# Long causal convolution beside attention: kv stationary in four column tiles, filter rows moving

## The chip, the cores and the metric

The kernel runs on one core of a Trainium2 chip. The metric is the device time of one execution in microseconds (us), the median of several runs. Every experiment is measured on the same chip as fresh runs of the kernel before.

## The reference, cut to what matters

Two independent branches are computed and laid side by side.

```python
# A (H3-style): short convolution of k, times v, then a causal convolution over all 2048 steps
for t in range(4):
    k_shift = k_shift + k_pad[:, t:t + S, :] * shift_k[:, 3 - t]
kv = k_shift * v                                   # [2048, 640]
y = irfft(rfft(kv_pad) * rfft(ssm_k_pad))[:S]      # y[s] = sum_r kv[r] * ssm_k[s - r], each of 640 channels
a = q * (y + kv * ssm_D)
# B: full (not causal) attention, 32 heads of 20, with its projections
p = softmax((q @ k.T) * 20 ** -0.5);  b = (p @ v) @ wo
out = concat([a, b], -1)                           # [1, 2048, 1280]
```

## The kernel before

The program is straight-line code. A planner in Python, with an assumed cost for each operation, orders the instructions of all engines at build time: attention is the frame, the projections and the convolution are put into gaps that the planner sees on TensorE.

The exponentials are shared between ScalarE (two or three score tiles an instruction) and VectorE (one tile as a chain of five instructions), which gets a tile when its planned backlog is short:

```python
def EXP_task(k, m, vec, b0, got):                       # m tiles on ScalarE, vec (0 or 1) on VectorE
    P.op("act", lambda e: e.activation(P_sb[:, s0:s0 + m, :], ..., ACT.Exp, scale=scale), ...)
    if vec:
        chain_start(k + m, b0 + m, got[m])
def want_vec(k, now):
    if not 60 < k < NU - 34 or len(chains) >= NXB or not xfree: return 0
    if ((k + 2) // 4) % NKB > 13 or micro_late(now - 1.5): return 0
    return int(max(0.0, P.T["dve"] - now) + backlog() < VQ)
```

The convolution is a set of matmuls with a Toeplitz matrix. One filter tile `HK` serves four channels; its columns are the stationary operand and kv, spread over zeros by GpSimd, moves. The cost in the code is what the planner assumes; in the trace of this kernel the convolution's matmuls start 25 ns apart at 8 columns, 29 at 64 and 55 at 128 (medians at full clock):

```python
def hk_load(qd):      # 4 transfers of 32 partitions, one 4224-byte run each
    P.dmas("sp", [(HK[...][32 * X:32 * X + 32], ap(kext, [[1, 32], [1, HKW]], ...)) for X in range(4)], ...)
def kvx_build(c):     # 80 copies in all
    P.op("pool", lambda e: e.tensor_copy(dst, src), ...)
def conv_task(bt):    # 40 tasks of 4 x 32 matmuls
    lhsT = HK[sl][:, 64 + 128 * d - 32 * r1:64 + 128 * d - 32 * r1 + 128]   # 128 neighbouring elements
    rhs = sub(KVX[i], [[128, 2], [1, n]], ...)                              # 8 to 128 columns
    cost = max(0.025, 2 * n / 2400 + 0.0025)
    # [...] then three VectorE instructions to take the sums out
```

The softmax here doesn't subtract the row's maximum and nothing guards it: scores larger than these inputs give would overflow.

## Time and profile before

| | kernel before |
|---|---|
| time, three runs | 893.14 us median (888.44 to 895.65) |
| span of the profiled run | 889.3 us |
| ScalarE busy with exponentials / idle just before them | 851.5 / 19.1 us |
| VectorE chains of five instructions | 171 |
| TensorE instructions | 11,432 weight loads, 11,432 matmuls |
| half clock after 213 us (the trace's clock records) | 24 us |

"Idle" stands in the last column of a group's line: the time that the engine had nothing to do just before instructions of this group. A group that grows in busy time with the same count has slower instructions; a group that grows in idle time is waiting. Three groups from the page of the kernel before, to be held against the same groups later; other lines are in the prediction:

```profile
L639 ACT ACTIVATE P_sb<-PS 128x1536 bf16<-128x1536 f32 (+1 forms) x729 | 851.5, 1417 | 19.1 <-PE PS L597 18.4
...
L931 PEld LDWEIGHTS PS<-R 128*128 128x128 bf16 x5120 | 197.7, 97 | 108.9 <-issue 108.5
...
L668 DVE SCALAR_TENSOR_TENSOR XZ<-XI 128x512 f32<-128x512 uint16 x171 | 123.0, 719 | 0.4
```

### The profile page before, as it was taken

The numbers are of one execution on the slowest core, as the hardware profiler recorded it, in microseconds if no ns is written. First come the engines' busy times: TensorE is split into PE (matmuls) and PEld (weight loads), VectorE is DVE, ScalarE is ACT, GpSimd is POOL, SyncE is SP. The second block draws the span as 40 slices with busy tenths as digits, with TensorE's granted clock in tenths as the row PEclk, the third lists the DMA queues.
The fourth block names the chain that finished last, engine by engine and source line by source line (L and its number), as shares of the span: only waits on it lengthen the run. The fifth ranks groups of instructions, "written<-read, shape, count | busy, mean of one in ns | idle before, by whom it ended". The sixth has DMA issues, their size and how long they took to land.

```text
span 889.3 us, 26279 instructions
## 1 busy us (share of the span) xinstructions
PE 835.4 (94%) x11432; PEld 388.0 (44%) x11432; DVE 785.4 (88%) x1427; ACT 856.0 (96%) x737; POOL 126.5 (14%) x94
## 2 busy tenths in 40 slices
PE   9999889998999999998999999999989999999987
PEld 5432223222455554544545454444545445454322
DVE  4569999999699999998999999899999999999752
ACT  6699999999799999998999999999999999999996
POOL 3000000001522021210220220122022012200000
PEclk9999999999699999999999999999999999999999
DMA  9614233335666675553579656675644546355141
GB/s 301 202 56 153 93 116 105 105 105 90 158 176 175 176 191 140 158 138 99 161 161 180 162 162 187 177 210 146 169 131 131 163 130 190 110 162 145 32 107 56
DMA packets 83598, 129.15 MB, mean 145 GB/s; under 512 B 34561, under 2 KB 60283, under 8 KB 83483
## 3 DMA queue, kind: packets, MB, share of 16 engines
q1 hardware_dynamic: 81323, 124.36, 51.0%
q0 software_dynamic: 704, 2.74, 1.0%
q8 instruction: 90, 1.47, 0.7%
q10 hardware_dynamic: 1456, 0.37, 0.2%
q14 instruction: 25, 0.20, 0.1%
HBM read 116.81 MB, written 13.23 MB: 146 GB/s over the span
## 4 chain that ended last, share of the span: by engine, by line
ACT 48%; DVE 30%; PE 20%; issue 1%; DVEq 0%
ACT P_sb L639 48%; PE PS L931 7%; PE PS L597 6%; DVE P_sb L673 5%; DVE XI L666 5%; DVE XZ L668 5%; DVE XZ L671 5%; DVE XI L670 4%; PE PS L692 3%; PE PS L445 2%; DVE R L952 1%; PE PS L348 1%; DVE ZS L950 1%; DVE ZS L949 1%; DVE OT_sb L702 1%
## 5 line engine op out<-in xcount | busy, mean ns | idle before, releaser
L639 ACT ACTIVATE P_sb<-PS 128x1536 bf16<-128x1536 f32 (+1 forms) x729 | 851.5, 1417 | 19.1 <-PE PS L597 18.4
L597 PE MATMUL PS<-QT,KT 20*128 20x512 bf16 x2048 | 286.5, 388 | 30.6 <-ACT P_sb L639 21.7
L931 PE MATMUL PS<-R 128*128 128x128 bf16 (+15 forms) x5120 | 245.1, 194 | 3.6 <-DVE R L952 2.5
L931 PEld LDWEIGHTS PS<-R 128*128 128x128 bf16 x5120 | 197.7, 97 | 108.9 <-issue 108.5
L692 PE MATMUL PS<-P_sb,V_sb 128*21 128x512 bf16 x2048 | 173.5, 388 | 6.0 <-DVE P_sb L673 4.8
L901 POOL COPY R<-R 32x512 bf16<-32x512 bf16 x80 | 114.9, 1436 | 443.7 <-PE PS L931 431.3
L597 PEld LDWEIGHTS PS<-QT,KT 20*128 20x128 bf16 x2048 | 70.7, 91 | 200.1 <-ACT P_sb L639 153.8
L666 DVE TENSOR_SCALAR XI<-PS 128x512 int32<-128x512 f32 x171 | 117.0, 684 | 17.4 <-PE PS L597 16.8
L671 DVE SCALAR_TENSOR_TENSOR XZ<-XZ,XI 128x512 f32<-128x512 f32 x171 | 128.1, 749 | 0.0
L673 DVE SCALAR_TENSOR_TENSOR P_sb<-XZ,XI 128x512 uint16<-128x512 f32 x171 | 120.9, 707 | 4.9
L668 DVE SCALAR_TENSOR_TENSOR XZ<-XI 128x512 f32<-128x512 uint16 x171 | 123.0, 719 | 0.4
L670 DVE TENSOR_SCALAR XI<-XI 128x512 int16<-128x512 int16 x171 | 93.2, 545 | 0.0
L692 PEld LDWEIGHTS PS<-P_sb,V_sb 128*21 128x21 bf16 x2048 | 37.6, 89 | 79.4 <-issue 50.4
L348 PE MATMUL PS<-Zt 128*128 128x512 bf16 x208 | 63.6, 402 | 1.5 <-DVE Zt L342 1.0
L530 DVE TENSOR_TENSOR R<-R 128x640 bf16<-128x640 bf16 x128 | 61.6, 487 | 3.7 <-DMA R<-in_A_v_dram 0.9
L445 PE MATMUL PS<-xT,WQ 128*20 128x512 bf16 (+1 forms) x660 | 48.9, 385 | 3.6 <-DVE R L952 1.7
L445 PE MATMUL PS<-xT,R 128*20 128x512 bf16 (+2 forms) x660 | 44.8, 374 | 0.2
L702 DVE CAST OT_sb<-PS 128x512 bf16<-128x512 f32 x32 | 21.9, 685 | 14.5 <-PE PS L692 14.2
L503 PE MATMUL PS<-R,xT 128*128 128x160 bf16 (+1 forms) x240 | 31.2, 257 | 1.6 <-ACT P_sb L639 0.8
L431 DVE CAST KT<-PS 128x512 bf16<-128x512 f32 (+1 forms) x32 | 21.4, 673 | 11.1 <-PE PS L445 11.1
L878 POOL MEMSET R<- 128x2048 bf16 x2 | 3.8, 1900 | 190.7 <-DMA kvr_scratch<-R 190.6
L431 DVE CAST QT<-PS 128x512 bf16<-128x512 f32 (+1 forms) x32 | 21.6, 676 | 6.3 <-PE PS L445 6.2
(52 smaller groups left out, 302.0 us busy)
## 6 DMA issues: line engine op xcount, KB each, us to landing
R<-kext_scratch SPq DMA_DIRECT2D x640, 132.0 KB, 3.0
R<-in_A_k_dram SPq DMA_DIRECT2D x15, 640.0 KB, 3.9
kext_scratch<-in_A_ssm_k_dram POOLq DMA_DIRECT2D x1, 2560.0 KB, 14.7
R<-in_A_v_dram SPq DMA_DIRECT2D x16, 160.0 KB, 5.4
kv_scratch<-R SPq DMA_DIRECT2D x16, 160.0 KB
kvr_scratch<-R SPq DMA_DIRECT2D x16, 160.0 KB
R<-kvr_scratch SPq DMA_DIRECT2D x8, 320.0 KB, 7.0
R<-in_A_q_dram SPq DMA_DIRECT2D x32, 80.0 KB, 2.0
```

What stands on the lines that cost most here:

```text
L348: P.op("pe", lambda e: e.matmul(bank[bk], Zt, zrhs, start=start, stop=start, skip_group_check=True), reads=[b_Zt], writes=[bkb[bk]], tok=s ...
L445: ins = e.matmul(bank[bk][32 * i:32 * i + DH, 0:n], Wt[:, cc, off + i * DH:off + (i + 1) * DH], xT[:, cc, x0:x0 + n], start=(cc == 0), sto ...
L597: ins = e.matmul(bank[b0 + i], KT[32 * u:32 * u + DH, g, kb * 128:(kb + 1) * 128], QT[32 * u:32 * u + DH, qs(qc, g), :], start=True, stop= ...
L639: P.op("act", lambda e: e.activation(P_sb[:, s0:s0 + m, :], PS[:, b0 * 512:(b0 + m) * 512].rearrange("p (u q) -> p u q", u=m), ACT.Exp, sc ...
L666: (lambda e: e.tensor_scalar(XI, bank[bk], scale * 1.4426950408889634 * w, 127.0 * w, op0=ALU.mult, op1=ALU.add), [bkb[bk]], [bl, bh], 0.6 ...
L668: (lambda e: e.scalar_tensor_tensor(XZ, u, w * c2 / c3, u, op0=ALU.add, op1=ALU.mult), [bl], [bz], 0.69, True),
L670: (lambda e: e.tensor_scalar(hi, hi, 128.0, None, op0=ALU.mult), [bh], [bh], 0.456, True),
L671: (lambda e: e.scalar_tensor_tensor(XZ, XZ, w * w * c1 / c3, u, op0=ALU.add, op1=ALU.mult), [bl, bz], [bz], 0.69, True),
L673: (lambda e: e.scalar_tensor_tensor(P_sb[:, z, :].bitcast(U16), XZ, 128.0 * c3 / w ** 3, hi, op0=ALU.mult, op1=ALU.add), [bh, bz], [b_P[z] ...
L692: ins = e.matmul(bank[OBANK][32 * u:32 * u + DH + 1, :], V_sb[:, kb, 4 * g + u, :], P_sb[:, slot[4 * b + u], :], start=first, stop=last, t ...
L901: P.op("pool", lambda e, dst=dst, src=src: e.tensor_copy(dst, src), reads=[cv["KVr"]], writes=[cv["KVX"][i]] if X == 3 else [], extra=(cv[ ...
L931: P.op("pe", lambda e, o=o, lhsT=lhsT, rhs=rhs, st=st, last=last: e.matmul(o, lhsT, rhs, start=st, stop=last, skip_group_check=True), read ...
```

## The change

The intent: the convolution loads 128x128 weights 5120 times for only 8 to 128 moving columns each, GpSimd's copies cost VectorE time (L671 takes 753 ns in the mean from 240 to 830 us and 679 from 780 to 830, where GpSimd rests), and taking sums out costs three VectorE instructions a task. So the operation is turned round: kv becomes the stationary operand, 32 columns for one channel, four channels in the four column tiles of the array; 64-column pieces of the filter rows move. Four far offsets of 512 steps fill the 128 rows of the contraction. GpSimd's copies go, sums leave by one copy, a transpose and one addition, and gating is done inside each task. The diff cut to its core (`[...]` marks cuts):

```diff
+HKW = 544
+NHK = 3
+CB, NJ, J0, NT = 64, 78, 14, 20
+CQ = 0.03
+PVMIN, TIGHT = 3, 9
[...]
-        def kvx_build(c):                     # GpSimd's copies
[...]
+        def kva_load(b):
+            P.dmas("sp", [(sub(KVA, [[2 * CB, 64 - 16 * a], [1, CB]], (J0 + 16 * a) * 2 * CB + CB * h, 32 * a, 32),
+                           ap(kvr_d, [[D, 32], [32 * D, 64 - 16 * a], [1, CB]], h * D // 2 + b * CB))
+                          for a in range(4) for h in range(2)], d_kva, reads=b_kvd, writes=[cv["KVA"]])
+        def hk_load(gi):                      # 4 transfers, runs of 1088 bytes
+            P.dmas("sp", [(HK[i][32 * a:32 * a + 32].rearrange("p (c x) -> p c x", c=8),
+                           ap(kext, [[1, 32], [KXL, 8], [1, HKW]], [...] + 512 * a)) for a in range(4)], [...])
+        def conv_task(t):                     # 20 tasks x 4 x 2 x 16 groups
+                            for j in range(4):
+                                ins = e.matmul(
+                                    bank[bk][32 * j:32 * j + 32, (2 * v + h) * 64:(2 * v + h) * 64 + 64],
+                                    sub(KVA, [[4 * CB, 32]], (J0 - 2 * d + r) * 2 * CB + h * CB + t % 4 * 16 + 4 * v + j),
+                                    HK[i][:, (4 * w + j) * HKW + 64 * d - 32 * r + 32:(4 * w + j) * HKW + 64 * d - 32 * r + 96],
+                                    start=st, stop=sp, tile_position=(0, 32 * j), skip_group_check=True)
+                        P.op("pe", pe, reads=rd, writes=[bkb[bk]], tok=last, c=CQ, st=64 / 2400, kind="pv")
+            [...] copy to SBUF, Y_task: transpose, add kv * D, multiply by q
-                m = min(len(ok), 2 if slack < 1.0 else 3)
+                m = min(len(ok), max(1, int((slack + 0.1) / 0.22)))
```

In `sub(KVA, [[4 * CB, 32]], ...)` the 32 weights of a tile lie 4 x 64 = 256 elements, 512 bytes, apart. In `KVA` the channels lie side by side, because that is how kv can be transferred in runs of 128 bytes.

More of the change, by code (lines that the diff above doesn't have):

```diff
@@ L23 @@
 KXL = S + KPAD
-HKW = 2112
-NHK = 4
+HKW = 544
+NHK = 3
+CB, NJ, J0, NT = 64, 78, 14, 20
 NPU = 24
@@ L275, in build_kernel @@
         Wo_sb = sb("Wo_sb", [128, NCC, D])
-        Dbc = sb("Dbc", [128, D])
+        Dh = sb("Dh", [128, D // 2])
         ident = sb("ident", [128, 128])
-        ZS = sb("ZS", [128, 256], FP32)
         rden = sb("rden", [128, 32], FP32)
-        HK_E, KVR_E, KVX_E, Y_E, AST_E = HKW, 64 * 80, 8 * 256, 16 * 320, 320
+        HK_E, KVA_E, A_E = 8 * HKW, NJ * 2 * CB, 32 * CB
         ph0 = NCC * 2 * D + 4 * 4 * D + 2 * 5 * D + KS * D + 2 * D + 2 * D
-        ph1 = NHK * HK_E + KVR_E + 2 * KVX_E + 2 * Y_E + 5 * AST_E
+        ph1 = NHK * HK_E + KVA_E + 2 * 512 + 2 * A_E
         xT = sb("xT", [128, NCC, S])
@@ L301, in build_kernel @@
         HK = [carve(HK_E) for _ in range(NHK)]
-        KVr = carve(KVR_E).rearrange("p (j c) -> p j c", j=64)
-        KVX = [carve(KVX_E) for _ in range(2)]
-        Y = [carve(Y_E).rearrange("p (t c) -> p t c", t=16) for _ in range(2)]
-        Aq = [carve(AST_E) for _ in range(3)]
-        Akv = [carve(AST_E) for _ in range(2)]
+        KVA = carve(KVA_E)
+        Ys = [carve(512) for _ in range(2)]
+        Akv, Aq = carve(A_E), carve(A_E)
         PS = E(nc.psum_tensor("PS", [128, 4096], FP32))[:, :]
@@ L316, in build_kernel @@
         kvr_d = nc.dram_tensor("kvr_scratch", (S, D), BF16).ap()
-        b_ident, b_ones, b_tA, b_tB, b_C, b_ZS = (Buf() for _ in range(6))
+        b_ident, b_ones, b_tA, b_tB, b_C = (Buf() for _ in range(5))
         b_WK0, b_WQ0, b_Wa, b_Wb, b_Wo, b_D = (Buf() for _ in range(6))
@@ L559, in setup_pool @@
             P.op("pool", lambda e: e.memset(V_sb[:, :, :, DH:DH + 1], 1.0), writes=[b_ones])
-            P.op("pool", lambda e: e.memset(ZS, 0.0), writes=[b_ZS])
             P.op("pool", lambda e: e.memset(kst[0][0:KS - 1, 0:KS, :], 0.0), writes=[b_kst[0]])
@@ L570, in setup_pool @@
             P.dma("sp", Wo_sb, ap(B_wo, [[D, 128], [128 * D, NCC], [1, D]]), d_small, writes=[b_Wo])
-            P.dma("sp", Dbc, ap(A_ssm_D, [[0, 128], [1, D]]), d_small, writes=[b_D])
+            P.dmas("sp", [(Dh[64 * h:64 * h + 64], ap(A_ssm_D, [[0, 64], [1, D // 2]], h * D // 2)) for h in range(2)], d_small,
+                   writes=[b_D])
             kst_load(0)
@@ L864, in build_kernel @@
         d_hk = [DS("hk%d" % i) for i in range(NHK)]
-        d_aq = [DS("aq%d" % i) for i in range(3)]
-        d_ao = [DS("ao%d" % i) for i in range(3)]
+        d_kva, d_akv, d_aq, d_ao = DS("kva"), DS("akv"), DS("aq"), DS("ao")
         def conv_setup():
@@ L870, in conv_setup @@
             cv["HK"] = [Buf(*allx) for _ in range(NHK)]
-            cv["KVr"] = Buf(*allx)
-            cv["KVX"] = [Buf(*allx) for _ in range(2)]
-            cv["Y"] = [Buf(*allx) for _ in range(2)]
-            cv["Aq"] = [Buf(*allx) for _ in range(3)]
-            cv["Akv"] = [Buf(*allx) for _ in range(2)]
-            cv["Z"] = [Buf(b_ZS), Buf(b_ZS)]
-            for i in range(2):
-                P.op("pool", lambda e, i=i: e.memset(KVX[i], 0.0), writes=[cv["KVX"][i]], c=1.9)
-            kvr_load(0)
@@ L880, in conv_setup @@
-            for qd in range(NHK):
-                hk_load(qd)
-            kvx_build(0)
-            kvx_build(1)
-        def kvr_load(B):
-            P.dmas("sp", [(KVr[32 * X:32 * X + 32], ap(kvr_d, [[D, 32], [32 * D, 64], [1, 80]], 320 * B + 80 * X))
-                          for X in range(4)], d_kvr, reads=b_kvd, writes=[cv["KVr"]])
-        def hk_load(qd):
-            B, m = divmod(qd, 80)
-            P.dmas("sp", [(HK[qd % NHK][32 * X:32 * X + 32],
-                           ap(kext, [[1, 32], [1, HKW]], (320 * B + 80 * X + m) * KXL + 1)) for X in range(4)],
-                   d_hk[qd % NHK], reads=[b_kext], writes=[cv["HK"][qd % NHK]])
@@ L895, in kvx_build @@
-        def kvx_build(c):
-            B, cl = divmod(c, 10)
-            i = c % 2
-            for X in range(4):
-                dst = sub(KVX[i], [[256, 8], [64, 4], [4, 16]], X, 32 * X, 32)
-                src = sub(KVr, [[1, 8], [80, 4], [320, 16]], cl * 8, 32 * X, 32)
-                P.op("pool", lambda e, dst=dst, src=src: e.tensor_copy(dst, src), reads=[cv["KVr"]],
-                     writes=[cv["KVX"][i]] if X == 3 else [], extra=(cv["KVX"][i].r + cv["KVX"][i].w) if X == 0 else (), c=1.35)
-            if cl == 9 and B == 0:
-                kvr_load(1)
@@ L906, in conv_reads @@
-        def conv_reads(bt):
-            rd = []
-            for qd in range(4 * bt, 4 * bt + 2):
-                rd += [cv["HK"][qd % NHK], cv["KVX"][(qd // 8) % 2]]
-            return rd
-        def conv_task(bt):
-            B, j = divmod(bt, 20)
-            for u in range(4):
-                qd = bt * 4 + u
-                c, ql = divmod(qd, 8)
-                i = c % 2
-                sl = qd % NHK
-                for d in range(16):
-                    for r1 in range(2):
-                        n = (16 - d) * 4
-                        first = (d == 0 and r1 == 0)
-                        last = (d == 15 and r1 == 1)
-                        lhsT = HK[sl][:, 64 + 128 * d - 32 * r1:64 + 128 * d - 32 * r1 + 128]
-                        rhs = sub(KVX[i], [[128, 2], [1, n]], ql * 256 + r1 * 64)
-                        o = sub(bank[MISC], [[256, 2], [1, n]], u * 64 + d * 4)
-                        st = first and u == 0
-                        cost = max(0.025, 2 * n / 2400 + 0.0025)
-                        yield (cost, [cv["HK"][sl], cv["KVX"][i]] if first else [])
-                        P.op("pe", lambda e, o=o, lhsT=lhsT, rhs=rhs, st=st, last=last: e.matmul(
-                            o, lhsT, rhs, start=st, stop=last, skip_group_check=True),
-                            reads=[cv["HK"][sl], cv["KVX"][i]], writes=[bkb[MISC]], tok=last, c=cost,
-                            st=2 * n / 2400)
-                        if last:
-                            if qd + NHK < 160:
-                                hk_load(qd + NHK)
-                            if ql == 7 and c + 2 < 20:
-                                kvx_build(c + 2)
-            M, Yb = bank[MISC], Y[B]
@@ new lines, in conv_setup @@
+            cv["KVA"] = Buf(*allx)
+            cv["Ys"] = [Buf(*allx) for _ in range(2)]
+            cv["Akv"] = [Buf(*allx) for _ in range(4)]
+            cv["Aq"] = [Buf(*allx) for _ in range(4)]
+            n = (J0 + 48) * 2 * CB
+            P.op("pool", lambda e: e.memset(KVA[:, 0:n], 0.0), writes=[cv["KVA"]], c=n * 0.00095)
+            kva_load(0)
+            for gi in range(NHK):
+                hk_load(gi)
+            a_load(0)
+        def kva_load(b):
+            P.dmas("sp", [(sub(KVA, [[2 * CB, 64 - 16 * a], [1, CB]], (J0 + 16 * a) * 2 * CB + CB * h, 32 * a, 32),
+                           ap(kvr_d, [[D, 32], [32 * D, 64 - 16 * a], [1, CB]], h * D // 2 + b * CB))
+                          for a in range(4) for h in range(2)], d_kva, reads=b_kvd, writes=[cv["KVA"]])
@@ new lines, in a_rows, with a_load @@
+        def a_rows(t, w, b, h):
+            return ap(t, [[w, 64], [64 * w, 32], [1, CB]], h * D // 2 + b * CB)
+        def a_load(b):
+            for t, x, d, key, rd in ((kvd, Akv, d_akv, "Akv", b_kvd), (q2, Aq, d_aq, "Aq", [])):
+                P.dmas("sp", [(x[64 * h:64 * h + 64].rearrange("p (t c) -> p t c", c=CB), a_rows(t, D, b, h))
+                              for h in range(2)], d, reads=rd, writes=cv[key])
+        def hk_load(gi):
+            t, q = divmod(gi, 4)
+            c0 = q // 2 * (D // 2) + t * 16 + q % 2 * 8
+            i = gi % NHK
+            P.dmas("sp", [(HK[i][32 * a:32 * a + 32].rearrange("p (c x) -> p c x", c=8),
+                           ap(kext, [[1, 32], [KXL, 8], [1, HKW]], c0 * KXL + KPAD - 63 + 512 * a)) for a in range(4)],
+                   d_hk[i], reads=[b_kext], writes=[cv["HK"][i]])
@@ new lines, in conv_reads, with pe @@
+        def conv_reads(t):
+            return [cv["HK"][4 * t % NHK], cv["KVA"]]
+        def conv_task(t):
+            bk = MISC
+            for q in range(4):
+                gi = 4 * t + q
+                h, vp = divmod(q, 2)
+                i = gi % NHK
+                rd = [cv["HK"][i], cv["KVA"]]
+                for w in range(2):
+                    v = 2 * vp + w
+                    for k in range(16):
+                        d, r = divmod(k, 2)
+                        first, last = w + k == 0, w == 1 and k == 15
+                        def pe(e, h=h, i=i, w=w, v=v, d=d, r=r, st=q + w + k == 0, sp=k == 15):
+                            for j in range(4):
[4 more added lines that the diff above has]
+                                    start=st, stop=sp, tile_position=(0, 32 * j), skip_group_check=True)
+                            return ins
+                        yield (CQ, rd if first else [])
+                        P.op("pe", pe, reads=rd, writes=[bkb[bk]], tok=last, c=CQ, st=64 / 2400, kind="pv")
+                        if last and gi + NHK < 4 * NT:
+                            hk_load(gi + NHK)
+            if t % 4 == 3 and t + 1 < NT:
+                kva_load(t // 4 + 1)
+            y, by, sl = Ys[t % 2], cv["Ys"][t % 2], slice4(t)
+            work(1.4, [(lambda e: e.tensor_tensor(sl(Akv), sl(Akv), ap(Dh, [list(Dh.ap[0]), [0, 32], [1, 16]], t * 16), ALU.mult),
+                        [cv["Akv"][t % 4], b_D], [cv["Akv"][t % 4]], 0.33, True)])
+            work(0.8, [(lambda e: e.tensor_copy(y, bank[bk]), [bkb[bk]], [by], 0.69, False)],
+                 lambda: add(nu[0] // 4 + 4, 0.27, ("Y", t), lambda bk: Y_task(t, bk)))
@@ new lines, in slice4, with Y_task, pe @@
+        def slice4(t):
+            return lambda x: sub(x, [[CB, 32], [1, 16]], t % 4 * 16)
+        conv_done = [0]
+        def Y_task(t, bk):
+            y, by, sl = Ys[t % 2], cv["Ys"][t % 2], slice4(t)
+            yield (0.24, [by])
+            def pe(e):
+                for v in range(4):
+                    ins = e.transpose(bankh[bk][:, v * 128:(v + 1) * 128], y[:, v * 128:(v + 1) * 128], ident)
+                return ins
+            P.op("pe", pe, reads=[by, b_ident], writes=[bkb[bk]], c=0.24)
+            ka, kq = cv["Akv"][t % 4], cv["Aq"][t % 4]
+            b = t // 4
@@ L942, in after @@
             def after():
                 conv_done[0] += 1
-                if j == 19:
-                    micro.append([A_iter(B), None])
-                    mark[:] = [micro_n[0], P.T["pe"]]
-            y, bz = cv["Y"][B], cv["Z"]
-            work(0.8, [(lambda e: e.tensor_copy(ZS[64:128], M[0:64, 256:512]), [bkb[MISC]], [bz[0]], 0.425, False),
-                       (lambda e: e.tensor_copy(sub(ZS, [[64, 4], [1, 60]], 4, 0, 64), sub(M, [[64, 4], [1, 60]], 256, 64, 64)),
-                        [bkb[MISC]], [bz[1]], 0.41, False),
-                       (lambda e: e.tensor_tensor(sub(Yb, [[320, 16], [80, 4], [1, 4]], 4 * j),
-                                                  sub(M, [[4, 16], [1, 4], [64, 4]]),
-                                                  sub(ZS, [[4, 16], [1, 4], [64, 4]]), ALU.add),
-                        [bkb[MISC]] + bz, [y], 0.425, False)], after)
@@ L957, in build_kernel @@
-        conv_done = [0]
-        def A_load(B, tp):
-            i = tp % 3
-            o = tp * 128 * D + 320 * B
-            P.dmas("sp", [(Aq[i], ap(q2, [[D, 128], [1, 320]], o)), (Akv[tp % 2], ap(kvd, [[D, 128], [1, 320]], o))], d_aq[i],
-                   reads=b_kvd, writes=[cv["Aq"][i], cv["Akv"][tp % 2]])
-        def A_iter(B):
-            A_load(B, 0)
-            A_load(B, 1)
-            db = Dbc[:, 320 * B:320 * B + 320]
-            def tt(o, a, b, op, reads, writes):
-                P.op("dve", lambda e: e.tensor_tensor(o, a, b, op), reads=reads, writes=writes, c=0.327, two=True)
-            for tp in range(16):
-                i, h = tp % 3, tp % 2
-                q, k = cv["Aq"][i], cv["Akv"][h]
-                yield [k]
-                tt(Akv[h], Akv[h], db, ALU.mult, [k, b_D], [k])
-                yield []
-                tt(Akv[h], Y[B][:, tp, :], Akv[h], ALU.add, [cv["Y"][B], k], [k])
-                yield [q]
-                tt(Aq[i], Aq[i], Akv[h], ALU.mult, [q, k], [q])
-                P.dma("sp", ap(out2, [[2 * D, 128], [1, 320]], tp * 128 * 2 * D + 320 * B), Aq[i], d_ao[i], reads=[q])
-                if tp + 2 < 16:
-                    A_load(B, tp + 2)
@@ new lines, in after @@
+                if t % 4 == 3:
+                    P.dmas("sp", [(a_rows(out2, 2 * D, b, h), Aq[64 * h:64 * h + 64].rearrange("p (t c) -> p t c", c=CB))
+                                  for h in range(2)], d_ao, reads=cv["Aq"])
+                    if t + 1 < NT:
+                        a_load(b + 1)
+            work(1, [(lambda e: e.tensor_tensor(sl(Akv), sub(bankh[bk], [[1, 32], [32, 16]]), sl(Akv), ALU.add),
+                      [bkb[bk], ka], [ka], 0.69, False),
+                     (lambda e: e.tensor_tensor(sl(Aq), sl(Aq), sl(Akv), ALU.mult), [ka, kq], [kq], 0.33, True)], after)
@@ L1034, in reads_of @@
                 return [b_xT[key[1]], b_ones, b_Wa if key[2] == 0 else b_Wb], []
+            if k == "Y":
+                return [cv["Ys"][key[1] % 2]], []
             if k == "N":
@@ L1072, in micro_late @@
                 return micro_n[0] < (now - KV0) * KVPACE
-            return conv_done[0] == 40 or micro_n[0] - mark[0] < (now - mark[1]) * APACE
+            return conv_done[0] == NT or micro_n[0] - mark[0] < (now - mark[1]) * APACE
         mark = [0, 0.0]
@@ L1137, in conv_wants @@
         def conv_wants(now):
-            return conv_k is not None and conv_b < 40 and conv_b <= 40 * (nu[0] - conv_k) / (NU - CONVE - conv_k) + 0.5
+            return conv_k is not None and conv_b < NT and conv_b <= NT * (nu[0] - conv_k) / (NU - CONVE - conv_k) + 0.5
         def pick(limit, slack, now, bnow):
@@ L1197, in build_kernel @@
         half = 0
-        while nu[0] < NU or npv[0] < NB - 1 or conv_b < 40 or conv or side or pend or tail[0] < 2:
+        while nu[0] < NU or npv[0] < NB - 1 or conv_b < NT or conv or side or pend or tail[0] < 2:
             now = P.T["pe"]
@@ L1241, in build_kernel @@
             idle = not conv and not side
-            if tail[0] < 2 and not pend and idle and conv_b == 40 and P.ready("pe", b_OnT, [bkb[MISC]]) <= now + 0.05 and (
+            if tail[0] < 2 and not pend and idle and conv_b == NT and P.ready("pe", b_OnT, [bkb[MISC]]) <= now + 0.05 and (
                     k >= NU - 6 if tail[0] == 0 else k == NU and P.ready("pe", (), [bkb[2]]) <= now):
@@ L1254, in build_kernel @@
             if ok:
-                tight = len(free) < (6 if conv else 8)
-                m = min(len(ok), 2 if slack < 1.0 else 3)
-                if m >= 2 and not conv and slack > 0.55 or tight or nrem == 1 or k == NU or bnow < 6:
+                tight = len(free) < TIGHT
+                m = min(len(ok), max(1, int((slack + 0.1) / 0.22)))
+                if m >= PVMIN or tight and m >= min(2, nrem) or len(free) < 4 or nrem == 1 or k == NU or bnow < 6:
                     for b in ok[:m]:
@@ L1304, in build_kernel @@
         tail_tasks(2)
-        fin = [d[2] for d in d_B + d_ao + [d_Bs]]
+        fin = [d[2] for d in d_B + [d_ao, d_Bs]]
         waits = [(t[2], t[1]) for t in fin]
```

## The prediction

> **What bounds the kernel now.** I read the busy shares first, then the slices, the groups by form, the same groups stage by stage, and last the chain of waits.
>
> ```profile
> PE 835.4 (94%) x11432; PEld 388.0 (44%) x11432; DVE 785.4 (88%) x1427; ACT 856.0 (96%) x737; POOL 126.5 (14%) x94
> ...
> DVE  4569999999699999998999999899999999999752
> ACT  6699999999799999998999999999999999999996
> ...
> PEclk9999999999699999999999999999999999999999
> ```
>
> Three engines look full. ScalarE is the one without holes from the fourth slice on, except in slice eleven, where the granted TensorE clock falls too. ScalarE does little but the softmax exponentials:
>
> ```profile
> L639 ACT ACTIVATE P_sb<-PS 128x1536 bf16<-128x1536 f32 x419 | 607.5, 1618 | 6.0 <-PE PS L597 5.6
> L639 ACT ACTIVATE P_sb<-PS 128x1024 bf16<-128x1024 f32 x310 | 333.1, 1145 | 13.1 <-PE PS L597 12.8
> ...
> L931 PE MATMUL PS<-R 128*128 128x128 bf16 x320 | 46.8, 220 | 3.6 <-DVE R L952 2.5 <-DVE Bout L766 0.6 <-DVE Bside L766 0.3
> ...
> L931 PE MATMUL PS<-R 128*128 128x8 bf16 x320 | 31.9, 167 | 0.0
> ```
>
> There are 2048 score tiles of 128x512: 419 x 3 + 310 x 2 = 1877 on ScalarE, and 171 on VectorE as a five-instruction polynomial. The mean durations overlap, so I took the spacing of consecutive starts in the trace: 1.330 us for a triple, 0.904 for a pair. 419 x 1.330 + 310 x 0.904 = 837.5 of the 889.3 us. The time is therefore the number of triples and pairs, plus about 52 us in which ScalarE is late. A tile given to VectorE turns a triple into a pair and is worth 1.330 - 0.904 = 0.426 us.
>
> By stage (us, then busy time of PE, PEld, DVE, ACT, POOL, clock, DMA share, GB/s):
>
> ```profile
> 213.00:240.00 27.00, 25.69 (x226) 8.38 (x219) 17.76 (x23) 21.13 (x19) 14.79 (x10) 0.62 0.78 151
> 240.00:780.00 540.00, 514.60 (x7865) 269.53 (x7861) 513.97 (x889) 535.32 (x461) 103.57 (x72) 1.00 0.60 160
> 780.00:830.00 50.00, 48.07 (x724) 24.29 (x721) 49.30 (x89) 50.00 (x44) 0.00 (x0) 1.00 0.47 128
> 830.00:870.00 40.00, 34.85 (x269) 10.31 (x269) 23.55 (x63) 40.00 (x32) 0.00 (x0) 1.00 0.33 87
> ```
>
> Up to 213 us VectorE prepares kv; then the convolution runs until 830, and the second half of the gating by q follows it. In 830 to 870 VectorE is half idle, because the planner that orders all instructions at build time gives it no tile while gating is left over; the chain of waits there is ScalarE alone:
>
> ```profile
> 829.98 40.36 ACT P_sb L639 x31
> ```
>
> That is 29 triples and 2 pairs: 29 x 1.330 + 2 x 0.904 = 40.4. Counting starts in the trace, 780 to 830 passes 128 tiles (2.56 per us), 240 to 780 only 1309 (2.42), 830 to 870 only 91 (2.28). VectorE's groups say why (240 to 830, then 780 to 830, where GpSimd rests):
>
> ```profile
> L671 DVE SCALAR_TENSOR_TENSOR XZ<-XZ,XI 128x512 f32<-128x512 f32 x145 | 109.1, 753 | 0.0
> ...
> L670 DVE TENSOR_SCALAR XI<-XI 128x512 int16<-128x512 int16 x145 | 78.9, 544 | 0.0
> L952 DVE TENSOR_TENSOR R<-PS,ZS 128x256 bf16<-128x256 f32 x39 | 23.3, 598 | 1.2
> L949 DVE COPY ZS<-PS 64x256 f32<-64x256 f32 x39 | 16.3, 418 | 4.5 <-PE PS L931 3.4
> L950 DVE COPY ZS<-PS 64x240 f32<-64x240 f32 x39 | 16.0, 409 | 1.2
> ```
>
> ```profile
> L671 DVE SCALAR_TENSOR_TENSOR XZ<-XZ,XI 128x512 f32<-128x512 f32 x15 | 10.2, 679 | 0.0
> L670 DVE TENSOR_SCALAR XI<-XI 128x512 int16<-128x512 int16 x15 | 6.7, 449 | 0.0
> ```
>
> The same instruction takes 753 against 679 ns, 544 against 449: GpSimd's copies (80 of 1.44 us) cost VectorE time. So ScalarE bounds the kernel, VectorE decides how much ScalarE is spared, and TensorE, in order, makes ScalarE late now and then.
>
> [...]convolution matmuls start 55 ns apart at 128 columns, 25 ns apart at 8. [...]The four-tile projection groups of 128 columns[...]: four matmuls 3 to 4 ns apart, next group 55 ns later. No group of 64 columns is in the trace. [...]The trace shows 0.5 from 218.3 to 238.7 us and from 402.6 to 406.0.
>
> **The change, part by part.**
>
> *TensorE.* Removed: 5120 weight loads and matmuls; their starts fill 229 us, waits included. Added: 20 tasks x 4 x 2 x 16 = 2560 groups of four column tiles, 64 columns each. Half the columns of the projection groups: [...]29 ns, 75 us in all, and 20 x 4 transposes, some 5 us. Around 140 us of in-order work go. It is not on ScalarE's path, except through lateness. Part of it comes back as filler matmuls[...] (54 in 830 to 870, where no convolution runs).
>
> *VectorE, 240 to 830.* Removed: eviction 23.3 + 16.3 + 16.0 = 55.6 us; 48 of the 96 gating products, 15.4 us. Added, per task: a 128x512 eviction, 0.685 (as every 128x512 copy from PSUM here), an addition from PSUM, 0.685, and two products. These are 0.323 us at 320 columns and 0.487 at 640, so 0.42 at 512. Sum 2.21, times 20 = 44.2. Net 26.8; neighbours overlap (55.5 us of groups fill 49.3 us in 780 to 830), so 23.8 us of engine time.
> GpSimd's copies all go. Over four chain instructions: (753 - 679) x 145 + (719 - 683) x 146 + (708 - 690) x 146 + (544 - 449) x 145 = 32 us.
> VectorE's idle time in this stretch is 590 - 513.97 - 49.30 = 26.7 us; at the rate of 780 to 830 (0.7 in 50) it would be 8.3. With an earlier TensorE I take 12 of the 18.
> Together 68 us. A chain is 683 + 683 + 690 + 679 + 449 = 3184 ns, times 49.3 / 55.5 = 2.83 us. So 24 more chains x 0.426 = **10.3 us**.
>
> *End.* Gating now runs inside each task, so VectorE goes on taking tiles until 34 are left. By 830 us 1937 tiles are done; the next 77 at 2.56 instead of 2.28 per us: 33.8 - 30.1 = **3.7 us**.
>
> *ScalarE's lateness in the convolution.* 590 - (286 x 1.330 + 218 x 0.904) = 12.5 us. With less on TensorE, half: **6 us**.
>
> *The slow clock at 218 us.* 27 - (8 x 1.330 + 9 x 0.904) = 8.2 us lost. [...]an even chance that the new order avoids it: **4 us**.
>
> *DMA.* Filter bytes stay (640 x 132 KB against 320 x 272 KB), in packets of 1088 instead of 4224 B. Trace: 4224 B take 242 ns, 1024 B 48, 1280 B 65, 160 B 20. Estimate: 81,920 x 52 ns + 112,640 packets of 128 B (kv, gating operands, output) x 20 ns = 6.5 ms over 16 engines, 407 us of some 600: 66%, against 0.60 now. No bound, but the kv load of a block, 10,240 packets, takes 13 us where the planner reckons 6. At the first block TensorE may stand for it: **minus 3 us**.
>
> Sum: 10.3 + 3.7 + 6 + 4 - 3 = 21 us; 893 - 21 = 872.
>
> **Rivals.**
> 1. Weight loads do not pipeline. They now read one element in 256[...]. Were the four loads serial[...] a group is 107 ns, 274 us in all, 200 more than planned for; the planner keeps little TensorE idle, so ScalarE starves: 930 to 980. For it: no such load in the trace. Against: the projection groups' loads are 3 to 4 ns apart.
> 2. The bound does not move: only the added tiles count, neither lateness nor clock improves. 893 - 14 + 3 = 882, within 2%.
> 3. DMA waits take over: small packets arrive late at five block starts, 5 to 8 us each, TensorE stands in order and ScalarE with it: 890 to 905. For it: the 8.6 us that GpSimd waits for the kv load now. Against: between tasks there is time, as 20 tasks need under 5 us of TensorE each in some 28.
> 4. With fewer real matmuls the clock drops more often; 8 us per event of 20 us: 880 to 890.
>
> **Range and chances.** Main path 872. If VectorE fills as well as in 780 to 830 throughout, the 1514 tiles from 240 us to the last chain take 591 us at 2.56 instead of 590 + 34 = 624; with the slow clock gone too, about 852, the far good end. Rival 2 gives 882. Range 856 to 886. The 2% line is 875.3, near the centre, but a whole rewrite with its pacing retuned speaks for the better half: faster 0.60, same 0.34, slower 0.06.
>
> **What would show it.** Right: some 195 to 205 VectorE chains, the 16-bit chain instruction near 450 ns, GpSimd below 25 us busy, convolution groups 28 to 32 ns apart, chains until some 15 us before the last exponential, ScalarE still the longest in the chain of waits. Wrong: groups well over 35 ns (rival 1), ScalarE idle beside matmuls that wait for a load of R (rival 3), clock entries at 0.5 (rival 4), fewer than 185 chains (rival 2).

## More of the kernel before

All comparisons are between runs of the fast state; for a single run the state is unknown, which is said where it matters. No verdict here rests on less than 2 per cent.

## The result, and the profile after

The time is 1162.2 us (1158.65 to 1162.89, four runs), the kernel before beside it 892.12. The ratio is 1.302, interval 1.2959 to 1.3081. Ratios are the mean time of one kernel's fast runs over that of the other's of the same rounds, so not quite the ratio of the medians. 270 us are to be explained.

The busy shares and slices of the changed kernel's page:

```profile
PE 1042.0 (90%) x16882; PEld 550.0 (47%) x16892; DVE 1058.0 (91%) x1421; ACT 1128.4 (97%) x742; POOL 14.3 (1%) x12
...
ACT  5999999999999999999999999999999999999997
...
PEclk9999999999999989899999999999999999999999
```

ScalarE is still the engine without holes, and the clock is nearly full (0.983 granted in the mean). It has no more instructions than before (742 against 737). Its groups, and VectorE's, from the same page:

```profile
L639 ACT ACTIVATE P_sb<-PS 128x1536 bf16<-128x1536 f32 (+1 forms) x734 | 1123.8, 1827 | 17.3 <-PE PS L597 16.5
...
L921 PEld LDWEIGHTS PS<-R 128*32 128x32 bf16 x10240 | 338.0, 251 | 40.6 <-issue 34.5
L921 PE MATMUL PS<-R 128*32 128x64 bf16 x10240 | 351.5, 286 | 3.6 <-issue 1.6
...
L668 DVE SCALAR_TENSOR_TENSOR XZ<-XI 128x512 f32<-128x512 uint16 x197 | 211.8, 1075 | 0.5
...
L670 DVE TENSOR_SCALAR XI<-XI 128x512 int16<-128x512 int16 x197 | 117.6, 597 | 0.0
```

Read the busy column against the idle column. ScalarE's busy time rose by 1123.8 - 851.5 = 272.3 us, its idle time not at all (17.3 against 19.1). It does not wait for TensorE; its own instructions take longer. VectorE's L668, which neither reads nor writes PSUM, takes 1075 ns where it took 719 before, and 683 undisturbed. The convolution's loads last 251 ns each, where the kernel before shows 97, and its groups of four start 122 ns apart (median in the trace; the prediction had 29).

When this happens shows in a stretch of the timeline of the changed kernel (start and length in us, engine, line, operation, count):

```profile
299.21 16.92 ACT L639 ACTIVATE P_sb<-PS 128x1024 bf16<-128x1024 f32 x10
...
301.69 2.52 DVE L671 SCALAR_TENSOR_TENSOR XZ<-XZ,XI 128x512 f32<-128x512 f32 x1
...
302.18 2.06 PE L921 MATMUL PS<-R 128*32 128x64 bf16 x60
304.25 0.69 DVE L673 SCALAR_TENSOR_TENSOR P_sb<-XZ,XI 128x512 uint16<-128x512 f32 x1
```

Fifteen groups of convolution take 2.06 us. The VectorE instruction beside them takes 2.52 us instead of 0.68; the next one, when they are over, its usual 0.69. Ten pairs on ScalarE take 16.9 us instead of 10 x 0.904 = 9.0. Over the trace after 213 us, I sorted the exponentials by the share of their time with convolution instructions in flight. With no convolution beside them they took 1.03 times their spacing of before (1.330 or 0.904 us), whether the transfer engines were busy or not (the two cases differ by 2 per cent, with the engines' mean share under 0.2 and over 0.8); with more than three quarters, 3.10 times. The convolution is in flight for 361 us. So whatever it does holds up two other engines. L668 touches no PSUM; its operands lie in SBUF, like the convolution's weights; whether the hold-up arises there, the trace does not show.

### The profile page after: what moved, and what is told of

Same layout as the page of the kernel before. It is cut to its first block, busy times and chain, and to the rows that moved or that the text cites.

```text
span 1159.5 us, 36741 instructions
## 1 busy us (share of the span) xinstructions
PE 1042.0 (90%) x16882; PEld 550.0 (47%) x16892; DVE 1058.0 (91%) x1421; ACT 1128.4 (97%) x742; POOL 14.3 (1%) x12
## 4 chain that ended last, share of the span: by engine, by line
ACT 75%; DVE 12%; PE 9%; DMA 1%; SPq 1%; issue 1%; POOLq 1%; DVEq 0%
ACT P_sb L639 75%; PE PS L597 2%; DVE XZ L671 2%; DVE P_sb L673 2%; DVE XZ L668 2%; DVE XI L666 2%; PE PS L445 1%; PE PS L692 1%; PE PS L348 1%; DVE R L530 1%; PE PS L921 1%; DVE XI L670 1%; SPq L228 1%; DVE OT_sb L702 1%; POOLq L1296 1%
## 5 line engine op out<-in xcount | busy, mean ns | idle before, releaser
L639 ACT ACTIVATE P_sb<-PS 128x1536 bf16<-128x1536 f32 (+1 forms) x734 | 1123.8, 1827 | 17.3 <-PE PS L597 16.5
L921 PEld LDWEIGHTS PS<-R 128*32 128x32 bf16 x10240 | 338.0, 251 | 40.6 <-issue 34.5
L921 PE MATMUL PS<-R 128*32 128x64 bf16 x10240 | 351.5, 286 | 3.6 <-issue 1.6
L666 DVE TENSOR_SCALAR XI<-PS 128x512 int32<-128x512 f32 x197 | 192.0, 975 | 36.7 <-PE PS L597 35.3
L668 DVE SCALAR_TENSOR_TENSOR XZ<-XI 128x512 f32<-128x512 uint16 x197 | 211.8, 1075 | 0.5
L673 DVE SCALAR_TENSOR_TENSOR P_sb<-XZ,XI 128x512 uint16<-128x512 f32 x197 | 199.8, 1014 | 5.9
L671 DVE SCALAR_TENSOR_TENSOR XZ<-XZ,XI 128x512 f32<-128x512 f32 x197 | 190.8, 968 | 0.0
L348 PE MATMUL PS<-Zt 128*128 128x512 bf16 x468 | 141.6, 397 | 1.4 <-DVE Zt L342 1.0
L670 DVE TENSOR_SCALAR XI<-XI 128x512 int16<-128x512 int16 x197 | 117.6, 597 | 0.0
L348 PEld LDWEIGHTS PS<-Zt 128*128 128x128 bf16 x468 | 30.3, 99 | 55.7 <-issue 45.5
```

The lines of the kernel that those rows point to most:

```text
L348: P.op("pe", lambda e: e.matmul(bank[bk], Zt, zrhs, start=start, stop=start, skip_group_check=True), reads=[b_Zt], writes=[bkb[bk]], tok=s ...
L639: P.op("act", lambda e: e.activation(P_sb[:, s0:s0 + m, :], PS[:, b0 * 512:(b0 + m) * 512].rearrange("p (u q) -> p u q", u=m), ACT.Exp, sc ...
L666: (lambda e: e.tensor_scalar(XI, bank[bk], scale * 1.4426950408889634 * w, 127.0 * w, op0=ALU.mult, op1=ALU.add), [bkb[bk]], [bl, bh], 0.6 ...
L668: (lambda e: e.scalar_tensor_tensor(XZ, u, w * c2 / c3, u, op0=ALU.add, op1=ALU.mult), [bl], [bz], 0.69, True),
L670: (lambda e: e.tensor_scalar(hi, hi, 128.0, None, op0=ALU.mult), [bh], [bh], 0.456, True),
L671: (lambda e: e.scalar_tensor_tensor(XZ, XZ, w * w * c1 / c3, u, op0=ALU.add, op1=ALU.mult), [bl, bz], [bz], 0.69, True),
```

## The experiments

Fourteen kernels were run. Several are wrong. The comparison with the reference does not see the convolution's values, so says nothing about the convolution here, and nothing about the change's either. The two-tile kernels (e5, e13, e14) leave half of a PSUM tile unwritten. "Idle on issue" is TensorE's idle time before convolution matmuls (unless said otherwise) that the view of waits puts down to issue, that is, to nothing that the profile shows.

### e1, e2, e3, e4: the stride

Theory S: the strided weight loads are slow and hold up the others. Theory L: column tiles are slow to load whatever the stride. Theory D: the small transfer packets. Under S, S-bank stands for a harm that hangs on the particular distance, S-line for one that every gap does alike; both are only names, since no run shows a bank or a line.

e1, neighbouring weights:

```diff
-                                    sub(KVA, [[4 * CB, 32]], (J0 - 2 * d + r) * 2 * CB + [...]),
+                                    sub(KVA, [[1, 32]], (J0 - 2 * d + r) * 2 * CB + [...]),
```

> The change with its stationary operand read at 32 neighbouring elements in place of 32 elements 512 bytes apart; nothing else moves, the result is wrong on purpose. Theory S (the strided weight loads are what is slow[...]): groups of four column tiles fall from 121 to about 29-35 ns, the exponentials inside convolution stretches go back to 1.33 us a triple, time 860 to 885 us. Theory L (column tiles[...] are slow, whatever the stride): groups stay near 120 ns, time near 1160. Theory D (small transfer packets): unchanged, near 1160.

e2, rows padded by 8 elements, 544 bytes between weights (the convolution stays right):

```diff
+RW = 2 * CB + 8
[...]
-            P.dmas("sp", [(sub(KVA, [[2 * CB, 64 - 16 * a], [1, CB]], (J0 + 16 * a) * 2 * CB + CB * h, 32 * a, 32),
+            P.dmas("sp", [(sub(KVA, [[RW, 64 - 16 * a], [1, CB]], (J0 + 16 * a) * RW + CB * h, 32 * a, 32),
[...]
-                                    sub(KVA, [[4 * CB, 32]], (J0 - 2 * d + r) * 2 * CB + [...]),
+                                    sub(KVA, [[2 * RW, 32]], (J0 - 2 * d + r) * RW + [...]),
```

> The change with 8 elements of padding in each row of the stationary tile, so that its elements lie 544 instead of 512 bytes apart; correct result. Theory S-bank[...]: groups fall towards 30 ns and the time to 860-890 us, a correct version. Theory S-line[...]: unchanged, 1140 to 1170.

e3, weights 32 bytes apart:

```diff
-                                    sub(KVA, [[4 * CB, 32]], [...]),
+                                    sub(KVA, [[16, 32]], [...]),
```

> The change with its weights 32 bytes apart; wrong result on purpose. S-line: near 1160, as at 512 bytes. S-bank: between e1 and the change, since 32 elements then spread over 1 KB instead of 16 KB. Theory L: 1160.

e4, the kernel before with its 128 weights 32 bytes apart, no column tile in the convolution:

```diff
-                        lhsT = HK[sl][:, 64 + 128 * d - 32 * r1:64 + 128 * d - 32 * r1 + 128]
+                        lhsT = sub(HK[sl], [[16, 128]], d)
```

> The kernel before, with its 128-column weights read 32 bytes apart instead of side by side; wrong result on purpose. Theory S: stride alone does the harm, without any column tile: matmul starts 25-55 ns apart become 100 ns or more, exponentials stretch beside them, time 1200 to 1500 us. Theory L: near 893 us, since no column tile is added.

Measured: e1 1094.57 us (ratio 1.2228, interval 1.2131 to 1.2325), e2 1112.73 (1.2398, 1.2277 to 1.2520), e3 1113.37, e4 1107.35 (one run each). The times missed all my expectations but e3's, and that one was met by accident, since nothing of the hold-up is left in it. What the loads do, however, is settled. The groups of four start 29 ns apart in e1 at full clock, as the prediction had it, so theory L falls, and theory D with it, since e1 leaves all transfers as they are; 62 ns in e2 and e3; in e4 a single load of 128 weights with its matmul takes 62 ns too, where the median was 25 to 55 with neighbouring ones. VectorE and ScalarE are not held up by the convolution in any of the four (L668 takes 683 ns in e1 to e3, and 713 in e4, which has GpSimd's copies again; the kernel before has 719). For e2, from the groups by line (the numbers of lines are one higher in this kernel):

```profile
L640 ACT ACTIVATE P_sb<-PS 128x1024 bf16<-128x1024 f32 (+1 forms) x731 | 862.0, 1324 | 231.1 <-PE PS L598 229.0
...
L669 DVE SCALAR_TENSOR_TENSOR XZ<-XI 128x512 f32<-128x512 uint16 x196 | 133.8, 683 | 0.7
```

Eight elements of padding bring L668's 1075 ns (L669 here) back to 683, and ScalarE's busy time from 1123.8 to 862.0 us. So it is the distance of 512 bytes, and not a gap as such, that holds up the other engines. In this S-bank is right; as to the loads' own time both strides of 32 and 544 bytes cost the same doubled 62 ns, which is S-line. But now ScalarE is idle for 231 us, waiting for TensorE. One disease has been taken away and another is visible. The page of e1 shows it, with the clock line:

```profile
PEclk9999999998677867658786978887958868688999
...
L639 ACT ACTIVATE P_sb<-PS 128x1536 bf16<-128x1536 f32 (+1 forms) x734 | 859.4, 1323 | 214.3 <-PE PS L597 211.5
...
L921 PE MATMUL PS<-R 128*32 128x64 bf16 x10240 | 148.6, 215 | 97.9 <-issue 95.2
```

TensorE's clock is at half for 348 us after 213 us in e1, and TensorE is idle for 95 us on issue, 5.9 us at the longest. A stretch of e1's timeline, TensorE and ScalarE:

```profile
581.58 0.24 PE L921 MATMUL PS<-R 128*32 128x64 bf16 x3 [5.57 <-issue]
```

```profile
582.41 1.02 ACT L639 ACTIVATE P_sb<-PS 128x1024 bf16<-128x1024 f32 x1 [5.99 <-PE PS L597]
```

Counted in the trace, all 32 gaps of e1 over 1.5 us that are put down to issue, before any matmul (96.7 us together), end when TensorE has issued 185 to 194 instructions past a multiple of 256. The instruction queue's 16 KB transfers (pages, in the expectations below) come once in 256 instructions: the page of the change has 132 of them for 33,774 TensorE instructions, that of the kernel before 90 for 22,864. In the gap above one starts 2.65 us into the gap, takes 1.33 us, and TensorE resumes 1.6 us after it. In the tightest tenth of such intervals in e1 they are about 4 us apart, or some 64 instructions per us, while a burst of convolution would use eight in 29 ns. That this wait for instructions is what holds TensorE up is theory F, the supply of instructions. Against it stood theory C: the clock halves because the new convolution keeps TensorE's array less busy.

### e5, e6, e7, e8: supply or clock

e5 is e1 with `for j in range(2)` in place of `range(4)`.

> As e1 (neighbouring weights), but only two of the four column tiles of each group are issued: half the convolution's weight loads and matmuls, the same steps in the planner; wrong result on purpose. Theory F (TensorE runs out of instructions: a 256-instruction page takes about 4 us to arrive, and a burst uses one in about 1 us): the idle time put down to issue before the convolution falls from 95 us to under 20, the half clock from 348 us to under 150, time below 980 us. Theory C (the clock halves because the convolution streams too little, whatever the supply): with less streaming it halves as often or more, time 1080 to 1150.

e6, e7 and e8 are e1, e2 and the change with another cost in the planner:

```diff
-CQ = 0.03
+CQ = 0.1        # 0.12 in e8
```

> As e1, all four tiles, but the planner reckons 100 ns for a group in place of 30, so that a step waits for a longer gap and bursts are thinner (8 instructions per 100 ns at most); wrong result on purpose. Theory F: idle on issue under 30 us, time 880 to 950. Theory C: the planner also believes TensorE busier and puts in fewer filler matmuls, so the clock halves at least as much: 1080 or more.

> As e2 (544-byte stride, correct result) with 100 ns reckoned for a group. Theory F with the measured 62 ns a group: idle on issue under 30 us, time 880 to 960, perhaps near the kernel before. Theory C: 1100 or more.

> The change itself (512-byte stride) with 120 ns reckoned for a group, which is what it takes. If the loss came from the planner's wrong figure alone, 900 to 960 us. If the 512-byte weight loads hold up ScalarE and VectorE whenever they run (a 3.5-fold stretch over some 300 us of convolution), no plan helps: 1100 to 1200, with the stretch still there.

Measured: e5 940.01 us, idle on issue 5.1, half clock 140 us; e6 1025.91, 24.5 and 488; e7 1035.52 (ratio 1.1496, interval 1.1428 to 1.1565; the profiled run fell in the slow state), 19.0 and 451; e8 1294.14, 17.1 and 865. e5 is what theory F expects: half the instructions, groups still 29 ns apart, hardly any starving, 155 us less than e1. e6 and e7 show that both theories hold a part. With thinner bursts the idle time on issue fell to a quarter, as F wants, but the clock was at half for longer, as C wants: believing TensorE busier, the planner put in 222 filler matmuls instead of 468. They also ended with convolution left over: 78 and 85 us pass after the last exponential, where the kernel before has 9. e8's 1294 us lies above the 1100 to 1200 expected: the stretch stays (exponentials with half to three quarters of their time beside convolution took 1.6 times their spacing). The 3.5-fold over some 300 us in its expectation was an estimate; the trace of the change shows 3.10 and 361 us. Its last exponential ends at 1134 us, hardly before the change's 1151, and then 158 us more go on convolution that was left over. The clock was at half for 865 us, which no theory had foreseen; what that cost no run tells.

### e9, e10: groups handed out evenly

```diff
-            if can(conv, slack, now):
+            if can(conv, slack, now) and groups[0] <= 128 * NT * (nu[0] - conv_k) / (NU - CONVE - conv_k) + 6:
+                groups[0] += 1
                 conv = step(conv)
```

e9 is e2 with this and CQ = 0.063; e10 is e1 with this.

> 544-byte stride (correct result), 63 ns reckoned for a group, and the planner hands out the convolution's groups evenly over the scores (some 2 groups a score tile) in place of a task of 128 at a time. Instructions then come at about 52 per us against the 256 in about 4 us that arrive. Theory F (supply of instructions, then the clock): idle on issue under 20 us, half clock under 100 us, time 870 to 920. If the clock halves for lack of streaming by itself: 950 or more with little idle on issue.

> Neighbouring weights (wrong on purpose), 30 ns reckoned, groups handed out evenly. Theory F: the 95 us of idle on issue nearly gone, half clock under 100 us, 855 to 900 us, the time that the change was planned for. If not, 1000 or more.

Measured: e9 1020.7 us (ratio 1.1459, interval 1.1343 to 1.1575), idle on issue 30.7, half clock 295; e10 1002.28, 58.4 and 213. Better than e2 and e1, and far from expected. As I read the timeline of e10, an even plan does not stay even: once TensorE is late, it runs through what has piled up without the planned gaps, at the pace of the instruction supply. No run tests this reading.

### e11: 256 bytes

e11 is the change with `[[2 * CB, 32]]`, weights 256 bytes apart.

> The change with its weights 256 bytes apart; wrong result on purpose. If the hold-up of ScalarE and VectorE needs a stride of 512 bytes exactly: groups 62 ns, as at 32 and 544 bytes, no stretch, 1100 to 1120 us. If it comes with the number of elements that fall on the same part of the memory: between, groups of 62 to 121 ns and part of the stretch.

Measured: 1160.35 us, groups 122 ns apart, and VectorE as in the change:

```profile
L668 DVE SCALAR_TENSOR_TENSOR XZ<-XI 128x512 f32<-128x512 uint16 x197 | 207.8, 1055 | 0.5
```

So it is not 512 bytes alone, and not between: 256 does all the harm of 512, while 32 and 544 do none of it to the other engines. What it is in the distance that does it, the runs do not tell.

### e12, e13, e14: what is left

e12 is e1 without reloading the filter, `if last and gi + NHK < NHK` in place of `< 4 * NT`. e13 is e5 with the same. e14 is the change with two tiles of four.

> As e1 (neighbouring weights, four tiles), but the filter tiles are loaded three times only and then used again and again, so the 85 MB of filter packets in 1088-byte pieces are gone; wrong result on purpose. If late pages of instructions come from sharing the transfer engines with the filter: idle on issue falls from 95 to under 50 us and the time to 950-1030 us. If TensorE uses a page faster than one can arrive on idle transfer engines too: idle on issue stays over 70 us and the time over 1040.

> Neighbouring weights, half the tiles (half the convolution's instructions) and no filter reloads; wrong result on purpose. If stride, supply of instructions and waits for the filter are all there is, the planned time comes out: 855 to 885 us, half clock under 60 us. If the clock halves by itself for lack of streaming: 930 or more with little idle on issue or on transfers.

> The change itself (512-byte stride) with two of the four column tiles; wrong result on purpose. If each strided load holds up the others for its own length, half the loads cost half: the convolution's union falls from 361 to about 180 us, ScalarE's stretch with it, and the time to 1000 to 1060 us. If the hold-up comes from four tiles reading at once, it goes away: under 950.

Measured: e12 1014.22 us, idle on issue 69.8, half clock 202, which fits neither expectation as a whole. The filter's traffic makes it worse (the 16 KB transfers now come 3.4 us apart at the closest, against some 4), but 70 of the 95 us stay: about 75 instructions per us is the most that arrives in e12. e13 868.11, as its first expectation had it, beside 888.88 for the kernel before on the same chip. Its clock line, two groups and one stretch (us, then PE, PEld, DVE, ACT, POOL, clock, DMA share, GB/s):

```profile
PEclk9999999999999999999999999999999999999999
...
L639 ACT ACTIVATE P_sb<-PS 128x1024 bf16<-128x1024 f32 (+1 forms) x724 | 836.5, 1445 | 11.0 <-PE PS L597 10.8
```

```profile
L670 DVE TENSOR_SCALAR XI<-XI 128x512 int16<-128x512 int16 x199 | 90.8, 456 | 0.0
```

```profile
240.00:780.00 540.00, 493.12 (x8531) 199.87 (x8535) 521.37 (x921) 539.68 (x469) 0.00 (x0) 1.00 0.18 31
```

No idle on issue (0.2 us), no half clock (1.00 granted from 213 to 830 us), though this kernel streams half of e1's convolution columns. So the new convolution's thin use of the array does not by itself halve the clock. In e1 the drops come after idle gaps: TensorE is idle for at least 1.3 us of the 3.4 us before each of the 29 drops (3.413 us is the shortest clock record in the traces of the change and of the kernel before). With e13 this speaks against theory C as an explanation of e1; that the gaps bring the drops is my reading. It does not rule it out in general: in e4 the clock was at half for 331 us with under 1 us of idle on issue and almost no idle before most of the drops. There a load with its matmul took 62 ns; what brought those drops is not shown.

e14 988.7 us, half clock 116, which met neither expectation's time. The hold-up of the others is gone:

```profile
L639 ACT ACTIVATE P_sb<-PS 128x1536 bf16<-128x1536 f32 (+1 forms) x734 | 859.4, 1320 | 109.1 <-PE PS L597 105.8
...
L921 PEld LDWEIGHTS PS<-R 128*32 128x32 bf16 x5120 | 208.8, 178 | 45.7 <-issue 38.9
...
L668 DVE SCALAR_TENSOR_TENSOR XZ<-XI 128x512 f32<-128x512 uint16 x197 | 134.7, 684 | 0.5
```

So the hold-up shows with four of these loads beside each other (L668 at 1075 ns) and not with two (684). The loads stay slow: groups of two tiles start 75 ns apart (29 with neighbouring weights, e5), where the planner reckons 30, so TensorE is late and ScalarE idle for 109 us, here without any starving (0.0 us on issue). Two tiles with this stride are slow among themselves (75 ns); four are slow (122 ns) and hold up others too.

### The runs side by side

| kernel | time, us | groups apart, ns | ScalarE exponentials busy / idle, us | idle on issue, us | half clock after 213 us, us |
|---|---|---|---|---|---|
| before | 892.12 | | 851.5 / 19.1 | 0 | 24 |
| the change | 1162.2 | 122 | 1123.8 / 17.3 | 1.6 | 39 |
| e11, 256 bytes | 1160.35 | 122 | 1124.5 / 15.4 | 1.1 | 34 |
| e14, the change with half the tiles | 988.7 | 75 | 859.4 / 109.1 | 0.0 | 116 |
| e2, 544 bytes | 1112.73 | 62 | 862.0 / 231.1 | 73.1 | 297 |
| e1, neighbouring | 1094.57 | 29 | 859.4 / 214.3 | 95.2 | 348 |
| e12, and no filter traffic | 1014.22 | 29 | 851.4 / 142.6 | 69.8 | 202 |
| e5, e1 with half the tiles | 940.01 | 29 | 847.9 / 72.2 | 5.1 | 140 |
| e13, both | 868.11 | 29 | 836.5 / 11.0 | 0.2 | 0 |

What is left of e5 over e13 is 72 us: the profile of e5 has 20.7 us in which TensorE waits for filter tiles, up to 4.7 us at once, and half clock after such waits (140 us in all). That is rival 3 of the prediction, present but small.

No run gives a version that beats the kernel before with the whole convolution in it. The best complete one, e9, is 14.6 per cent slower. A complete one would need neighbouring weights, that is, kv transposed on the way, and half the instructions; this was not tried.

## Why the prediction was wrong

**Step "TensorE", the term 2560 x 29 ns = 75 us.** This is the first step that failed. 122 ns were measured instead of 29, and the convolution is in flight for 361 us. The prediction held the figure up with the projection groups, whose weights lie side by side, and carried it over to weights 512 bytes apart. e1 shows that 29 ns is right for neighbouring weights and e2 and e3 that a gap of 544 or 32 bytes doubles it. The kernel before has 29 ns between its convolution's 64-column matmuls too, and their weights also lie side by side. Rival 1 had the group's length nearly right (its 107 ns was an estimate of mine) but for another reason, four loads in a row; e1's four loads do pipeline, 29 ns from group to group. The sign named for rival 1, groups well over 35 ns, came true.

**"It is not on ScalarE's path, except through lateness."** False in the change, and this is the step through which the 270 us came; rival 1 shared the error. The loads lengthen ScalarE's and VectorE's own instructions, about threefold where four tiles' loads run beside them: 272 us more busy time on ScalarE, none more idle. The check I had named, "ScalarE idle beside matmuls", would have missed it. The lateness that rival 1 expected is what e2 shows, after the padding has taken the hold-up away.

**VectorE's relief.** Right in kind, buried in size. The change has 197 chains (195 to 205 predicted), GpSimd is at 14.3 us (below 25 predicted), the two products take 424 and 422 ns (0.42), copy and addition 685 and 693 (0.685). The 16-bit instruction is at 448 ns in its median, but 597 in the mean, because of the same hold-up.

**DMA.** The DMA share was 0.58 to 0.73 in the convolution's stretches up to 1000 us, 66 per cent predicted. The agreement is luck: a 1088-byte packet took 82.5 ns in the mean, not 52, a 128-byte one 13, not 20, which makes 514 us for each of the 16 engines where 407 were reckoned, and only the longer stretch hides it. In the planned 600 us it would have been some 86 per cent (an estimate from these numbers). What the prediction did not see is that instructions are transferred too (132 transfers of 16 KB in the page of the change), and that the filter's traffic delays them (e1 against e12, some 4 against 3.4 us apart): 20,480 convolution instructions instead of 10,240 on TensorE, in bursts of eight per 29 ns. It counted the time of instructions and not their number. In the change this cost next to nothing (1.6 us idle on issue), since its groups use eight instructions in 122 ns where e1's use them in 29; without the stride it is, by my reading of e5 (155 us less than e1 with half the instructions), the larger part of e1's 200 us over the kernel before, the 348 us at half clock included.

**The sum of 21 us.** The gains can be read where the three costs are away. e13 took 868.11 us against 888.88, 20.8 less, with 199 chains, 240 to 780 us passed at 2.49 tiles per us (2.42 before), the slow clock at 218 us gone. It does half of the convolution's work and one run is no interval, so it fits the predicted sum without proving it: half of the convolution's loads and matmuls and nearly all filter transfers are missing too, and that the totals agree may be luck.

**Rival 4** (clock): small in the change (39 us at half clock), large as soon as the stride is mended (297 us in e2, 348 in e1). It is not settled why the change itself, whose groups start 122 ns apart, keeps its clock, while e4, where a load with its matmul takes 62 ns, was at half for 331 us; no run tells. The 0.5 from 218.3 to 238.7 us and from 402.6 to 406.0 in the prediction is the granted clock in the trace of the kernel before.

## What to carry to other kernels

Before an operand's layout is turned round, look at the distance between the elements that one partition of it reads, on the stationary side too: neighbours, a gap of 32 or 544 bytes, and one of 256 or 512 bytes cost 29, 62 and 122 ns here for a group of four loads, and the last slowed ScalarE and VectorE beside it. Count TensorE's instructions per microsecond as well as their time, since here no more than some 64 (e1) to 75 (e12) per us arrived, and TensorE stood idle on issue for 95.2 and 69.8 us. When one group's busy time grows with its count unchanged and its idle time not, look for what runs beside it and not for what it waits for; and when one cause is removed and the time hardly moves, read the new profile from the start, because another cause may have been hidden behind it.
